# Two attention and dense layers on one core: a third query buffer, averages computed in pairs, and low parts moved to VectorE

## The chip, the core and the metric

The kernel runs on one core of a Trainium2 chip. The metric is the device time of one execution in microseconds; the figure for a version is the median of its runs. A core has a matrix engine, TensorE (PE, with its weight loads listed as PEld), and three engines for elementwise work, VectorE (DVE), ScalarE (ACT) and GpSimd (POOL). SyncE (SP) issues the DMA transfers between the memory off the core (HBM) and the core's own. Each engine takes its instructions in order and waits on semaphores for the others.

## What is computed

Two layers, each of two residual steps, on `x` of 2048 x 640 in fp32, with 32 heads of width 20 and a dense width of 1536:

```python
def _A_ref(x, wqkv, w_phi, wo):
    qkv = (x @ wqkv).reshape(B, S, 3, H, Dh) -> q, k, v per head
    pq = einsum("bhsd,hdf->bhsf", q, w_phi); pk likewise
    phi_q = concatenate([softmax(pq), softmax(-pq)], axis=-1)
    phi_k = concatenate([softmax(pk), softmax(-pk)], axis=-1)
    kv = einsum("bhsf,bhsd->bhfd", phi_k, v)
    z = sum of phi_k over s
    num = einsum("bhqf,bhfd->bhqd", phi_q, kv)
    den = einsum("bhqf,bhf->bhq", phi_q, z)[..., None] + 1e-6
    return (num / den) as rows @ wo

def _B_ref(x, w1, b1, w2):
    h = x @ w1 + b1
    return (h * tanh(softplus(h))) @ w2

x = x + _A_ref(_layernorm(x), ...)
x = x + _B_ref(_layernorm(x), ...)
(and the same two steps once more, with the same weights)
```

## The kernel before

**Numbers.** Each fp32 operand of a large matrix product is kept as a high part, its rounding to the matrix engine's format, and a low part, the rest (`operand - high`). A product is three matmuls: high by high, high by low weight, low by high weight. So every weight and every chunk of activations is split once: ScalarE copies the high part, another engine subtracts to get the low part. For weights that is `make_parts` (L152, subtraction at L155 on GpSimd), called by the generator `make_five` (L198), which gives out five row groups of weights one by one. For activations it is `Transposed.step` (copy and subtraction at L295 and L296 on VectorE), which gives two chunks of 128 columns at a time; `all()` does the steps that are left.

**Tiles and stages.** The rows go in 8 blocks (`NB`) of 2 tiles of 128 rows (`BT`). A layer has three stages.

1. `attend_first` (about 20 to 262 us in layer 1, 712 to 943 in layer 2). For each tile of rows it makes queries, keys and values. `queries` and `keys` project (L354), and `features` turns the result into the features: ScalarE copies it out of PSUM into a buffer `e`, VectorE finds a maximum and a minimum per head (L384), one subtraction is done on GpSimd for queries (L385) and on VectorE for keys, then come the exponential on ScalarE, the sum and its reciprocal on VectorE (L393, L394) and the scaling on GpSimd (L395). A query's features are transposed by VectorE (L439) and stored in HBM, `e_d`, by four DMAs on SP (L443). A key's features are multiplied with the values on PE and summed in one PSUM tile over all keys (L430).
   These generators are advanced a step at a time (`pending`, `advance`), so that the steps of several tiles interleave.
   The buffer `e` of a query comes from `query_tile`: two tiles, used in turn, in the place of weights that are not needed yet. The buffer of a key is one of the five `big` tiles (`big_tile`).
   Before the last block's fourth projection, `load(0)` starts the reading of block 0's query features into two `big` tiles (L548) and a smaller one.
2. `attend_second` (262 to 368 us, and 943 to 1051). `finish_kv` makes the summed products ready. For each tile, `average` multiplies the query features with them (L589, 44 matmuls, into a two-bank PSUM tile of `mm_tile`, of which there are two), and VectorE divides: sums to `den` (L598), their reciprocals (L599), the product (L602). The averaged rows of a block are turned by ten PE transposes (L290, within `Transposed.step`) and multiplied with `wo`: `Rows(b, t).half(c, ps)` is one half of the columns of one tile (15 matmuls, L354), after which VectorE adds the residual (L619) and takes statistics. PE and SP follow here the order in which the code is written (`manual_schedule`). The PSUM tiles of one bank come from `one_tile`, a ring of four.
3. `dense` (368 to 712 us, and 1051 to 1398). A step is a block and a pair of hidden chunks (six pairs a block): `hidden` (L697, 60 matmuls into a `one` tile) and `mish`, which is spread over ScalarE (L710, L714, L715, L722), VectorE (L712, L713, L717 to L721) and GpSimd (L723); some steps later `contract` (L739) multiplies its result with W2. In the first six steps the last five row groups of W2 are split, one a step (`last_w2`, L776). The normalized rows of the next block are read turned from HBM (`load_turned`) and split (`nxt.all()`) in the last step of a block.

**Order.** Outside stage 2 a scheduler with a model of time sets the order within each engine, bounded by the dependences, by the rings of buffers and by `issue_after`, which puts an instruction behind a named one. ScalarE's instructions that go through `act(...)` keep the order in which they are written.

Of the kernel before, what the change touches and what calls it, by code (L numbers as in the profile page):

```python
# [8 lines left out]
F32 = mybir.dt.float32  # L9
# [39 lines left out]
def kernel(  # L49
# [22 lines left out]
    def mm_tile():  # L72
        return psum.tile([P, 2, 512], F32, tag="mm", name="mm", bufs=2)
# [75 lines left out]
            c0 = c1  # L149
        return raw  # L150

    def make_parts(w, raw, ordered=False):  # L152
        for st, cs in raw:
            (act if ordered else nc.scalar.activation)(w[0][:, cs], st, AF.Copy)
            nc.gpsimd.tensor_tensor(w[1][:, cs], st, w[0][:, cs].bitcast(F32), op=ALU.subtract)  # L155

    def five_spares(j):

# [5 lines left out]
    def r2_wide(j, dtype=F32R):  # L164
        return wts.tile([P, 2, D], dtype, tag=f"r2{j}", name=f"r2{j}")
# [29 lines left out]
            nc.sync.dma_start(wp_d[1, s, k], kv_ws[k][s][:, :FW].bitcast(F32))  # L195
            nc.sync.dma_start(wp_d[0, s, k], q_ws[k][s][:, :FW].bitcast(F32))

    def make_five(j, rows):  # L198

        spares = five_spares(j)  # L200
        raws = [fetch_rows(rows(k), [spares[k]()]) for k in range(3)]
        yield
        for k in range(5):
            w = r2_pair(j + k)
            make_parts(w, raws[k])
            if k in (0, 1):
                raws.append(fetch_rows(rows(3 + k), [spares[3 + k]()]))
            yield w
# [156 lines left out]
        return g % 4, 2 * DH * (3 * (g // 4) + j)  # L365

    def query_tile(i):
        return r2_wide(10 + i % 2, F32).rearrange("p s d -> p (s d)")

    def features(ps, e, pool_sub):  # L370

# [197 lines left out]
    def attend_second(x_src, x_dst, acc, fetches, makes, fetch_next, begin_next):  # L569
        kva, o_ws, loaded, rest = acc  # L570
        rows = {}
        div = [None]

        def tail():

            with tc.issue_after(div[0]):
                next(rest, None)

        def average(b, t):

            phs = loaded[b]
            po = mm_tile()
            for g in range(G):
                n = 120 if g < 10 else 80
                w = GW if g < 10 else 42
                c, j = divmod(g, 8)
                for q in range(2):
                    s0 = t * P + 64 * q
                    nc.tensor.matmul(  # L589
                        po[64 * q:64 * q + 64, c, GW * j:GW * j + w], phs[g][:n, s0:s0 + 64],  # L590
                        kvb[:n, g, :w], start=True, stop=True)
            o = row_tile()
            den = work.tile([P, H], F32, tag="r", name="den", bufs=2)
            pv = [po[:, c, :(DH + 1) * n].rearrange("p (h d) -> p h d", d=DH + 1)
                  for c, n in ((0, 24), (1, 8))]
            hh = (slice(0, 24), slice(24, H))
            for c in range(2):
                nc.vector.tensor_scalar_add(den[:, hh[c]], pv[c][:, :, DH], DEN_EPS)  # L598
            nc.vector.reciprocal(den, den)  # L599
            for c in range(2):  # L600
                n = hh[c].stop - hh[c].start
                ins = nc.vector.tensor_tensor(o.rearrange("p (h d) -> p h d", d=DH)[:, hh[c]], pv[c][:, :, :DH],  # L602
                                        den[:, hh[c]].unsqueeze(2).to_broadcast([P, n, DH]), op=ALU.mult)
                div[0] = ins.ins
            rows.setdefault(b, []).append(o)
            if t == BT - 1:
                del loaded[b]

        class Rows:


            def __init__(self, b, t):
                self.t, self.xt, self.ps = t, xs[b], None
                self.bn = work.tile([P, 2, 6], F32, tag="bn", name="bn", bufs=2)

            def half(self, c, ps):
                project_half(ps, cur, self.t, o_ws, 0, c)
                part = self.xt[:, self.t, c * HC:(c + 1) * HC]
                nc.vector.tensor_tensor(part, ps[:, :HC], part, op=ALU.add)  # L619
                nc.vector.bn_stats(self.bn[:, c], part)  # L620

            def mean(self):
                mv = work.tile([P, 2], F32, tag="mv", name="mv", bufs=3)
                nc.vector.bn_aggr(mv, self.bn)
                return mv

        with tc.manual_schedule(engines={mybir.EngineType.PE, mybir.EngineType.SP}):
            kv = finish_kv(kva)
            next(rest)
            next(kv)  # L630
            loaded[1] = load(1)
            xs = {0: fetch(x_src, 0)}
            fetches[0]()
            next(rest)
            next(kv)
            next(rest)
            average(0, 0)
            average(0, 1)
            loaded[2] = load(2)
            average(1, 0)  # L640
            cur = Transposed(rows.pop(0)).all()
            average(1, 1)
            loaded[3] = load(3)
            for b in range(NB):
                if b == NB - 1:
                    ahead.all()
                elif b:
                    average(b + 1, 0)
                r0, r1 = Rows(b, 0), Rows(b, 1)
                r0.half(0, one_tile())  # L650
                if 0 < b < NB - 1:
                    average(b + 1, 1)
                tail()
                if b + 1 < NB:
                    xs[b + 1] = fetch(x_src, b + 1)
                if 0 < b and b + 3 < NB:
                    loaded[b + 3] = load(b + 3)
                if b == NB - 3:
                    fetch_next()
                r0.half(1, one_tile())  # L660
                mv0 = r0.mean()
                if b == NB - 2:
                    ahead = begin_next()
                py = mm_tile()
                r1.half(0, py[:, 0])
                if b + 1 < NB:
                    nxt = Transposed(rows.pop(b + 1)).all()
                r1.half(1, py[:, 1])
                norm_scale(b, [mv0, r1.mean()])
                xt = xs.pop(b)  # L670
                nc.sync.dma_start(row_block(x_dst, b), xt)
                makes[b]()
                if b + 1 < NB:
                    fetches[b + 1]()
                tail()
                if b < NB - 1:
                    cur = nxt
            for _ in rest:
                pass
        return ahead  # L680


    def dense(x_src, x_dst, w1s, w2s, first, last):
# [89 lines left out]
                ahead[t] = row_tile()  # L773
                nc.sync.dma_start(ahead[t], row_block(x_src, b)[:, t, :])

        last_w2 = make_five(KD, lambda k: w2[(7 + k) * P:(8 + k) * P, :])  # L776
        n_pr = KF // 2
        steps = [(b, pr) for b in range(NB) for pr in range(n_pr)]
        acts = {}
# [1 line left out]
        for i in range(len(steps) + SKEW):  # L781
            if i < len(steps):
# [5 lines left out]
                if pr == 3 and (b + 1 < NB or not last):  # L788
                    nxt = load_turned(n1_d[b + 1] if b + 1 < NB else n2_d[0], (v_tile, v_tile, row_tile))
                acts[i] = hidden(b, pr)  # L790
                if pr == 1 and b + 1 < NB:
                    with tc.issue_after(exps[0]):
                        normalize(b + 1, ahead, ahead)
                    spill_turned(ahead, n1_d[b + 1])
# [103 lines left out]
```

## Time and profile before

| | us |
|---|---|
| runs | 1399.83, 1400.14, 1402.13 |
| median | 1400.14 |
| the profiled execution | 1399.85 |
| its span | 1397.9 |
| its mean granted TensorE clock | 0.994 |

Busy time in the stages of the profiled execution, in us:

| stage | length | PE | DVE | ACT | POOL |
|---|---|---|---|---|---|
| layer 1, first phase (20 to 262) | 242 | 238.07 | 202.03 | 104.37 | 106.49 |
| second phase (262 to 368) | 106 | 105.09 | 79.67 | 27.98 | 40.08 |
| dense (368 to 712) | 344 | 342.32 | 274.60 | 171.87 | 90.49 |
| layer 2, first phase (712 to 943) | 231 | 220.08 | 201.10 | 89.95 | 103.36 |
| second phase (943 to 1051) | 108 | 107.33 | 79.79 | 28.46 | 40.79 |
| dense (1051 to 1398) | 347 | 340.73 | 243.23 | 156.69 | 75.49 |

The ends of the stages are read from where their first matmuls begin and are rounded. Times in rows of the profile are microseconds from the start of the span. A timeline row has the start, the duration, the engine, the line of the kernel, the operation, the tile written and the tiles read with their shapes, and how many instructions the row stands for; what is in brackets at its end is the idle time of the engine before it and what it waited for. A row of the waits has the engine, the tile and the line that waited, what it waited for, the total, the count and the longest. A row of the windows has busy time and count of each engine. A row of the groups has the busy time of all its instructions and the mean of one in ns.

### The profile page before, as it was taken

Reading aid. Unit: us, or ns where it says so; the run is one execution under the profiler, and the core shown is the slowest. Engines: PE = TensorE matmul, PEld = TensorE weight load, DVE = VectorE, ACT = ScalarE, POOL = GpSimd, SP = SyncE. Lnnn points to the kernel's source line nnn. Section 1 sums busy time; section 2 is a strip of 40 time slices with the busy share of each in tenths; the row PEclk is TensorE's granted clock in tenths of the full one; section 3 lists DMA queues with packets and bytes.
Section 4 is the critical chain, followed back from the end, with each engine's and each line's share of the span. In section 5 each row is a group of like instructions: output and inputs, shape, how many; then the busy total and the mean of one; then the engine's idle time right before and its main releaser. Section 6 shows DMA issues by size and latency. Waiting matters only on the chain. (4 is left out here: it accounts for less than half of the span.)

```text
span 1397.9 us, 30903 instructions
## 1 busy us (share of the span) xinstructions
PE 1364.9 (98%) x12866; PEld 1345.4 (96%) x12866; DVE 1089.6 (78%) x1814; ACT 587.7 (42%) x1035; POOL 460.1 (33%) x344
## 2 busy tenths in 40 slices
PE   7999999999999999999999999999999999999998
PEld 7989999999999999999999999989999999999998
DVE  5798877886688887788769899988667766777775
ACT  4444434222445454545443343432134544444443
POOL 1443543353442222222234544453344211211112
PEclk9999999999999999999999999999999999999999
DMA  8532434788624432344472433458965212333200
GB/s 312 156 60 63 88 51 93 201 242 290 207 62 95 114 96 65 73 107 104 137 229 56 91 67 58 67 118 268 279 236 177 74 26 71 95 95 95 68 28 20
DMA packets 350277, 169.03 MB, mean 121 GB/s; under 512 B 287097, under 2 KB 323689, under 8 KB 350137
## 3 DMA queue, kind: packets, MB, share of 16 engines
q1 hardware_dynamic: 350137, 167.06, 44.4%
q8 instruction: 101, 1.65, 0.5%
q14 instruction: 39, 0.32, 0.1%
HBM read 104.43 MB, written 62.59 MB: 119 GB/s over the span
## 5 line engine op out<-in xcount | busy, mean ns | idle before, releaser
L739 PE MATMUL mm<-r2h,ol 128*128 128x320 f32 x1280 | 305.4, 309 | 1.4 <-ACT ol L722 0.9
L723 POOL TENSOR_TENSOR ol<-big,ol 128x512 fp32r<-128x512 f32 (+1 forms) x98 | 130.6, 1333 | 458.1 <-ACT ol L722 393.0
L697 PE MATMUL one<-xtl,r1h 128*128 128x256 f32 x960 | 268.6, 280 | 2.0 <-DVE xtl L296 2.0
L697 PE MATMUL one<-xth,r1l 128*128 128x256 f32 x960 | 268.0, 279 | 0.0
L697 PE MATMUL one<-xth,r1h 128*128 128x256 f32 x960 | 266.5, 279 | 0.0
L739 PEld LDWEIGHTS mm<-r2h,ol 128*128 128x128 f32 x1280 | 219.1, 188 | 2.8 <-POOL ol L723 1.5
L739 PE MATMUL mm<-r2l,ol 128*128 128x320 f32 x640 | 197.3, 309 | 0.0
L354 PE MATMUL mm<-r1h,xth 128*128 128x304 f32 (+1 forms) x600 | 186.7, 311 | 6.8 <-ACT r L122 6.8
L354 PE MATMUL mm<-r1h,xtl 128*128 128x304 f32 (+1 forms) x600 | 185.4, 309 | 2.3 <-DVE xtl L296 2.2
L354 PE MATMUL mm<-r1l,xth 128*128 128x304 f32 (+1 forms) x600 | 185.5, 309 | 0.0
L697 PEld LDWEIGHTS one<-xtl,r1h 128*128 128x128 f32 x960 | 180.4, 188 | 2.7 <-DVE xtl L296 2.5
L697 PEld LDWEIGHTS one<-xth,r1l 128*128 128x128 f32 x960 | 180.4, 188 | 0.0
L697 PEld LDWEIGHTS one<-xth,r1h 128*128 128x128 f32 x960 | 179.9, 188 | 0.0
L712 DVE TENSOR_SCALAR big<-big 128x512 f32<-128x512 f32 (+1 forms) x98 | 56.6, 578 | 112.9 <-ACT big L710 112.9
L354 PE MATMUL mm<-r2h,xth 128*128 128x304 f32 (+1 forms) x460 | 142.6, 310 | 0.0
L354 PE MATMUL mm<-r2h,xtl 128*128 128x304 f32 (+1 forms) x460 | 140.4, 305 | 0.0
L354 PE MATMUL mm<-r2l,xth 128*128 128x304 f32 (+1 forms) x460 | 140.2, 305 | 0.0
L395 POOL TENSOR_TENSOR r<-r,r 128x1280 f32<-128x1280 f32 x32 | 77.5, 2423 | 149.0 <-DVE r L394 126.7
L354 PEld LDWEIGHTS mm<-r1h,xth 128*128 128x128 f32 x600 | 114.0, 190 | 8.1 <-ACT r L122 7.3
L710 ACT ACTIVATE big<-one,b1s 128x256 f32<-128x256 f32 x192 | 80.6, 468 | 96.2 <-PE one L697 95.6
L714 ACT ACTIVATE big<-big,two 128x512 f32<-128x512 f32 (+1 forms) x98 | 70.1, 715 | 119.2 <-DVE big L713 116.7
L739 PEld LDWEIGHTS mm<-r2l,ol 128*128 128x128 f32 x640 | 120.2, 188 | 0.0
(130 smaller groups left out, 3031.6 us busy)
## 6 DMA issues: line engine op xcount, KB each, us to landing
e_d<-r SPq DMA_DIRECT2D x128, 160.0 KB, 4.0
big<-e_d SPq DMA_DIRECT2D x32, 640.0 KB, 7.3
x_d<-xt SPq DMA_DIRECT2D x23, 640.0 KB, 4.0
xt<-x_d SPq DMA_DIRECT2D x22, 640.0 KB, 4.9
n_d<-xn SPq DMA_DIRECT2D x176, 80.0 KB, 2.4
xt<-in_x SPq DMA_DIRECT2D x16, 640.0 KB, 5.1
xn<-x_d SPq DMA_DIRECT2D x28, 320.0 KB, 4.2
v<-n_d SPq DMA_DIRECT2D x30, 256.0 KB, 3.2
```

What stands on the lines that cost most here:

```text
L354: nc.tensor.matmul(ps[:, :w], a[:, sl], r, start=(k == 0 and n == 0), stop=(k == KD - 1 and n == 2))
L395: nc.gpsimd.tensor_tensor(eg, eg, r.unsqueeze(2).to_broadcast([P, 2 * H, DH]), op=ALU.mult)
L697: nc.tensor.matmul(ph[:, j, :], l, r, start=(n == 0), stop=(n == 3 * KD - 1))
L710: exps[0] = nc.scalar.activation(part(ta, 0)[:, j - js.start], ph[:, j, :], AF.Exp, bias=b1s[:, 2 * pr + j:2 * pr + j + 1]).ins
L712: nc.vector.tensor_scalar_min(e, e, E_CAP)
L714: nc.scalar.activation(r, n, AF.Ln, bias=two)
L723: nc.gpsimd.tensor_tensor(al[:, js], n, ah[:, js].bitcast(F32), op=ALU.subtract)
L739: nc.tensor.matmul(pys[t][:, c, :HC], l[:, j, sl], r, start=(f == 0 and n == 0), stop=(f == KF - 1 and n == 2))
```

## The change

It has four parts.

1. `query_tile`: queries go round three buffers in place of two. The third is a `big` tile (query tiles 2, 5, 8, 11 and 14); the other two are the same as before.
2. `attend_second`: in the loop, the averages of both tiles of block b + 1 are computed one behind the other, ahead of the first half of block b; before, the second tile's stood between the first and the second half of `r0`. The two halves of `r1` take two `one` tiles; before, they took the two banks of an `mm` tile.
3. `make_parts` and `make_five` get an argument that names the engine of the low parts; `last_w2` has them made on VectorE, all others stay on GpSimd.
4. `dense`: in block 0, the first step of `nxt` (the split of block 1's first two chunks) is written at the fifth pair; before, it was done with the others at the sixth.

```diff
-    def make_parts(w, raw, ordered=False):
+    def make_parts(w, raw, ordered=False, low=nc.gpsimd):
         for st, cs in raw:
             (act if ordered else nc.scalar.activation)(w[0][:, cs], st, AF.Copy)
-            nc.gpsimd.tensor_tensor(w[1][:, cs], st, w[0][:, cs].bitcast(F32), op=ALU.subtract)
+            low.tensor_tensor(w[1][:, cs], st, w[0][:, cs].bitcast(F32), op=ALU.subtract)
...
-    def make_five(j, rows):
+    def make_five(j, rows, low=nc.gpsimd):
...
             w = r2_pair(j + k)
-            make_parts(w, raws[k])
+            make_parts(w, raws[k], low=low)
...
     def query_tile(i):
-        return r2_wide(10 + i % 2, F32).rearrange("p s d -> p (s d)")
+        return big_tile() if i % 3 == 2 else r2_wide(10 + i % 3, F32).rearrange("p s d -> p (s d)")
...
                 elif b:
                     average(b + 1, 0)
+                    average(b + 1, 1)
                 r0, r1 = Rows(b, 0), Rows(b, 1)
                 r0.half(0, one_tile())
-                if 0 < b < NB - 1:
-                    average(b + 1, 1)
                 tail()
...
                 mv0 = r0.mean()
                 if b == NB - 2:
                     ahead = begin_next()
-                py = mm_tile()
-                r1.half(0, py[:, 0])
+                r1.half(0, one_tile())
                 if b + 1 < NB:
                     nxt = Transposed(rows.pop(b + 1)).all()
-                r1.half(1, py[:, 1])
+                r1.half(1, one_tile())
...
-        last_w2 = make_five(KD, lambda k: w2[(7 + k) * P:(8 + k) * P, :])
+        last_w2 = make_five(KD, lambda k: w2[(7 + k) * P:(8 + k) * P, :], nc.vector)
...
                 acts[i] = hidden(b, pr)
+                if b == 0 and pr == n_pr - 2:
+                    with tc.issue_after(exps[0]):
+                        nxt.step()
                 if pr == 1 and b + 1 < NB:
```

## The prediction

> **What bounds the kernel now.** I read the page's first lines, then the waits of TensorE (PE) sorted by total, then busy time in windows of 20 us around each of those waits, then the chain of waits inside one block of the second phase. The page first:
>
> ```profile
> span 1397.9 us, 30903 instructions
> PE 1364.9 (98%) x12866; PEld 1345.4 (96%) x12866; DVE 1089.6 (78%) x1814; ACT 587.7 (42%) x1035; POOL 460.1 (33%) x344
> ```
>
> PE is busy for 98% of the span. So a gain has two sources: a stop of PE that goes away, or PE work that becomes cheaper. Idle time on the other engines counts only where it ends in such a stop. The waits of PE (engine, tile, line, releaser: us in total, times, longest) that stand near code of the change:
>
> ```profile
> PE mm L354 <- ACT r L122: 6.8, 2, 3.8
> PE one L430 <- POOL big L395: 3.9, 2, 3.2
> PE mm L354 <- DVE xtl L296: 2.2, 2, 1.8
> PE one L697 <- DVE xtl L296: 2.0, 2, 1.0
> ```
>
> That is 14.9 us. The windows say what else such a stop costs (columns: window, its length, busy us and instructions of PE, PEld, DVE, ACT, POOL, granted clock, DMA share, GB/s):
>
> ```profile
> 80.00:100.00 20.00, 16.97 (x222) 15.80 (x221) 19.92 (x25) 5.08 (x9) 10.93 (x8) 0.91 0.36 58
> 740.00:760.00 20.00, 19.59 (x254) 19.09 (x253) 20.00 (x22) 7.83 (x13) 11.42 (x6) 1.00 0.08 21
> 760.00:780.00 20.00, 16.23 (x222) 15.73 (x221) 15.83 (x17) 5.12 (x10) 9.02 (x5) 0.91 0.55 103
> 860.00:880.00 20.00, 20.00 (x249) 19.63 (x248) 19.32 (x21) 9.17 (x15) 6.59 (x4) 0.92 0.24 44
> 940.00:960.00 20.00, 18.48 (x373) 17.85 (x374) 14.02 (x36) 3.52 (x7) 3.54 (x3) 0.91 0.93 289
> 400.00:420.00 20.00, 18.76 (x141) 18.14 (x140) 15.38 (x22) 9.08 (x17) 6.16 (x5) 1.00 0.00 1
> 1080.00:1100.00 20.00, 18.71 (x137) 17.88 (x136) 14.87 (x20) 9.19 (x19) 8.22 (x6) 1.00 0.00 1
> ```
>
> The granted clock falls to 0.91 or 0.92 in or after the windows with the four longest stops and is 1.00 in the windows with the 1.0 us stops. A clock of 0.91 over 20 us is (1 - 0.91) x 20 = 1.8 us of PE lost besides the stop, 0.92 is 1.6. So a long stop costs its length and some 1.7 more. The reader should also see DVE busy for 20.00 and 19.92 us in two windows: ahead of those stops VectorE itself has no room.
>
> **Averages together (parts of the second phase).** The chain of waits inside one block there (start, duration, engine, tile, line, matmuls):
>
> ```profile
> 946.70 2.72 PE mm L589 x88
> ...
> 953.97 4.60 PE one L354 x30
> ...
> 961.86 2.20 PE mm L354 x15
> 964.06 1.41 PE mm L589 x44
> 965.47 2.40 PE one L354 x15
> 967.88 1.41 PE mm L589 x44
> 969.29 2.40 PE one L354 x15
> 971.68 2.20 PE mm L354 x15
> 973.89 1.09 PE one L290 x10
> ```
>
> A block is PE from end to end: 2.20 + 1.41 + 2.40 + 1.41 + 2.40 + 2.20 + 1.09 = 13.11 us. An average that stands alone is 1.41 and each projection half behind one is 2.40, while a half behind another is 2.20. Two averages in a row are 2.72 (the x88 row), two halves in a row 4.60 (the x30 row). The change makes it 2.20 + 2.72 + 4.60 + 2.20 + 1.09 = 12.81, so 0.30 less. Six blocks of a layer have averages in the loop, so 12 x 0.30 = 3.6 us, all on the path. Bounds: 0 if the switch between the two matmul shapes costs as much when it is done once, and 12 x 0.40 = 4.8 if each of the two places is worth the full difference of 2.40 to 2.20.
>
> The same part takes r1's two halves from the `one` ring, 7 tiles a block in place of 5, over 4 buffers. The second half then needs the tile that r1's first half used three allocations earlier, and waits for VectorE's add of that half (L619). VectorE's rows there:
>
> ```profile
> 305.04 0.49 DVE L619 TENSOR_TENSOR xt<-mm,xt 128x320 f32<-128x320 f32 x1 [0.94 <-PE mm L354]
> ...
> 310.43 0.89 DVE L602 TENSOR_TENSOR xn<-mm,den 128x480 f32<-128x480 f32 x2
> ```
>
> The add waits for PE, starts at once and takes 0.49; what hides it is the ten transposes between the halves, 1.09 us. I price this at nothing, with 0.6 us to spare (1.09 - 0.49). If that cover goes, everything behind the second half on PE (the next block's averages) waits too; that is the third rival.
>
> **Low parts on VectorE and the early split (start of the dense phase).** Rows of the first blocks of layer 1 against a later one:
>
> ```profile
> 400.38 1.94 DVE L713 SCALAR_TENSOR_TENSOR big<-big 128x512 f32<-128x512 f32 x1
> 408.65 1.80 POOL L155 TENSOR_TENSOR r2l<-xn,r2h 128x640 fp32r<-128x640 f32 x1 [0.63 <-POOL ol L723]
> 408.95 2.05 DVE L296 TENSOR_TENSOR xtl<-v,xth 128x512 fp32r<-128x512 f32 x1
> 417.12 0.69 DVE L713 SCALAR_TENSOR_TENSOR big<-big 128x512 f32<-128x512 f32 x1
> ```
> ```profile
> L134 DVE TENSOR_TENSOR r1l<-xn,r1h 128x640 fp32r<-128x640 f32 x4 | 3.3, 817 | 0.0
> ```
>
> A subtraction L155 on GpSimd is 1.80 us, and VectorE instructions that run beside one stretch: L713 takes 1.94 in place of 0.69, L296 2.05. L296 is the split of block 1's first chunks, and PE's hidden matmuls wait 1.0 us for it in each layer (the L697 row of waits). Moved to VectorE the subtraction is 0.82 by the row of L134, five a layer, 4.1 us; VectorE is busy 15.38 of 20 us in that window, so 4.6 are free. And the first split comes one step earlier. So the stop should go, and smaller delays of the activations with it. PE lacks 20 - 18.76 = 1.24 us in the one window and 20 - 18.71 = 1.29 in the other. I take 2.5 us for both layers, that is all of it, since both causes are taken away. Bounds: 0, if the activations' own chain sets the stop, and on the losing side 5 x 0.2 us, when each subtraction of 0.82 falls between two steps of one activation and its cover is short by a quarter, so +1.
>
> **The third query buffer (first phase).** Queries took two buffers in turn; a buffer is free when the transposed features are stored to HBM. ScalarE's copy out of PSUM waits for that store, and PE for ScalarE. The rows at the stops and those ahead of two others:
>
> ```profile
> 91.16 1.47 DVE L384 TENSOR_REDUCE m<-r 128x32 f32<-128x640 f32 x2
> 93.42 1.26 PE L430 MATMUL one<-big,v 128*21 128x40 f32 x56
> 93.69 1.27 POOL L385 TENSOR_TENSOR r<-r,m 128x640 f32<-128x640 f32 x1
> ...
> 770.00 0.68 ACT L122 ACTIVATE r<-mm 128x608 f32<-128x608 f32 x1 [8.91 <-DMA e_d<-r]
> 770.86 1.55 DVE L384 TENSOR_REDUCE m<-r 128x32 f32<-128x640 f32 x2 [1.88 <-ACT r L122]
> ...
> 831.22 1.54 DVE L384 TENSOR_REDUCE m<-r 128x32 f32<-128x640 f32 x2 [2.33 <-ACT r L122]
> ...
> 916.89 1.54 DVE L384 TENSOR_REDUCE m<-r 128x32 f32<-128x640 f32 x2 [2.16 <-ACT r L122]
> ...
> 941.08 2.26 PE L430 MATMUL one<-big,v 128*21 128x40 f32 x128 [3.18 <-POOL big L395]
> ```
>
> With a buffer to spare the copy no longer waits for the store. What is late next is VectorE and GpSimd, which make the features of queries and keys alike. Place by place:
> - Layer 1, at 87 to 90 us (3.03 of the 6.8 us): VectorE is busy 19.92 of 20 there. In the changed order query 3's reductions (1.47 us) and its GpSimd subtraction (1.27) stand ahead of the sum of key tile 2, which PE needs for L430. PE would reach that matmul some 3 us earlier than at 93.42 and find its operand 1.5 us later than before. The stop moves more than it goes: I take 0.5, bounds 4.8 (3.03 and the dip of 1.8) and -2 (a stop that is longer by 1.5, rounded up).
> - Layer 2, at 767 (3.8 us): VectorE is full up to 760 and idles 1.88 just ahead of 770.86. That much can be won; I take 2.0, bounds 5.6 (3.8 and 1.8) and 0.
> - Layer 2, at 856 to 858 (1.8 us, xtl of L296): VectorE idled 2.33 us at 831 for the copy and had not made it up by 858. Without that idle time the split is 2.33 earlier and the stop of 1.8 is gone, with the dip of 1.6 in the window from 860: 3.4, bounds 3.4 and 0.
> - Layer 2, at 938 (3.18 us, key features): VectorE idled 2.16 at 917. I take 2.0, bounds 5.0 (with its dip of 1.8) and 0.
>
> The Trainium skill, "TensorE: Matmul & The Clock Gate", section on the HAM clock gate, has the clock halved only after an idle window of about 3.4 us. By that rule the 1.8 us stop at 858 would have no dip, and the gain there would be 1.8 in place of 3.4; the row of 860 to 880 shows 0.92 all the same, and I go by the row.
>
> **What the borrowed buffer delays.** Query tiles 2, 5, 8, 11 and 14 now take one of the five `big` tiles, which keys and the loads of features for the second phase use as well. So the ring turns faster, and the two loads for block 1 (L548) get their tiles later; the first, on SP, now stands behind the last stores of a query and waits for the matmul of the last key tile. Before:
>
> ```profile
> 261.02 0.38 SPq L548 DMA_DIRECT2D big<-e_d  x1
> ...
> 267.36 0.80 PE L589 MATMUL mm<-kvb,big 120*64 120x63 f32 x20 [0.43 <-PE mm L589]
> ```
> ```profile
> big<-e_d SPq DMA_DIRECT2D x32, 640.0 KB, 7.3
> ```
>
> Only the second half was issued at 261.02 and landed 7.3 us later, at 268.3, just in time. Now both halves start then, with 640 KB more in flight; at the 289 GB/s of the window 940 to 960 that is 2.2 us. PE reaches the first average of block 1 at 267.36, so it waits 0 to 3 us. I take a loss of 1.0, bounds 0 and 8 (a stop of about 2.2 and a dip of 1.8 in each layer). In layer 2 the average of block 1 has more room and I add nothing.
>
> **The sum.** 3.6 + 2.5 + 0.5 + 2.0 + 3.4 + 2.0 - 1.0 = 13.0 us off the profiled execution, which took 1399.85 (span 1397.9 and 1.95 around it): 1386.9. The median of the three runs is 1400.14, so 0.3 above; my forecast for the median is 1387.0.
>
> **The rivals.**
> - *The wait only changes its name.* VectorE bounds the first phase (20.00 and 19.92 busy), so that the third buffer lets ScalarE run ahead and PE stops as long for key features and splits. For it: the two windows. Against: VectorE's idle times of 1.88, 2.33 and 2.16, all for the copy. Then 3.6 + 2.5 - 1.0 = 5.1 remain: 1395.
> - *All stops vanish.* The four stops with their dips are 3.0 + 1.8, 3.8 + 1.8, 1.8 + 1.6 and 3.2 + 1.8 = 18.8; with 3.6 and 2.5 that is 24.9: 1375. Against: the full window up to 760, and GpSimd's place in the order of layer 1.
> - *Slower: r1's second half waits for its tile.* If VectorE's add of the first half stands behind both averages' divisions (two tiles by 0.89 and their smaller steps, some 3 us), the half stops for 3 + 0.49 - 1.09 = 2.4 us in each of 12 blocks, 29 us, and the time is 1416. It decides from 1.1 us a block (13 / 12). Against: the divisions can start as the averages end, and 4.60 + 2.20 us of halves come before that add.
> - *It doesn't do what it says:* the copies already had other reasons to wait. The releaser in the rows, the store of `e_d`, speaks against it; its time is that of the first rival.
>
> **How the numbers follow.** The forecast has 0.56, with a range of its own of 1382 to 1391; the wait that changes its name 0.22; all stops vanish 0.13; slower 0.09. A change under 0.2% (2.8 us) can't be told from none. The forecast and the third case are faster by more, and 0.15 of the first rival's 0.22; the rest of it, 0.07, is the same. So faster 0.84, same 0.07, slower 0.09. The range runs from 1378, half way into the case without stops, to 1397, past the first rival; it leaves out some 0.15.
>
> **What would show it.** In the profile after: averages as rows of x88 and halves as x45 in a block of 12.8 us; no wait of ScalarE for `e_d` at the four places; at 90 us a PE stop of some 3 us at L430 in place of L354; no wait of L697 for xtl at 410 and 1092, L713 near 0.7 at 400; windows after 860 at clock 1.00; a short wait for `big<-e_d` at 267. The forecast is wrong if PE's waits in the first phase keep their total, if L354 waits for L619 in the second phase, or if the averages' rows grow with their number.

## The result, and the profile after

| | before | after |
|---|---|---|
| median of the runs, us | 1399.99 (4 runs, 1398.67 to 1402.13) | 1382.85 (4 runs, 1381.50 to 1384.39) |
| span of the profiled execution, us | 1397.9 | 1380.6 |

The ratio is 0.9876, with a 95% interval of 0.9859 to 0.9894. That is 17.1 us less, where 13 were forecast; the time lies inside the range of 1378 to 1397. From here on, lines of the kernel after are two lower than before from the loop of `attend_second` on (L697 is L695, L713 is L711).

The page after, and the waits of TensorE (PE) near the changed code:

```profile
span 1380.6 us, 30853 instructions
PE 1356.1 (98%) x12866; PEld 1341.1 (97%) x12866; DVE 1082.9 (78%) x1824; ACT 586.5 (42%) x1035; POOL 442.0 (32%) x334
```
```profile
PE mm L354 <- DVE xtl L296: 3.6, 5, 1.4
PE mm L354 <- ACT xth L122: 2.6, 1, 2.6
PE one L430 <- POOL big L395: 1.6, 2, 0.9
PE mm L589 <- DMA big<-e_d: 0.8, 1, 0.8
```

The wait for ScalarE's copies of queries (6.8 us before) is gone, and so is that of the hidden matmuls for xtl, the low part of a chunk of activations (2.0). ScalarE's own 16 waits for the stores to `e_d` (74.9 us before) are gone too. The wait for a key's features is 1.6 in place of 3.9. New are 2.6 us for xth, the high part of a chunk; the projections' wait for xtl grew from 2.2 to 3.6 us, and that for a load from 0.2 to 0.8. So PE's stops of the first phases (for query copies, key features, xtl and xth) fell from 12.9 to 7.8 us and did not go. To find where the 17 us come from, take three matmuls that stand at the same place of both programs: the last product of keys and values of layer 1, the first projection of layer 2, and the last product of layer 2. First before, then after (timeline of PE; the row for 941.08 of before is in the prediction):

```profile
260.12 1.48 PE L430 MATMUL one<-big,v 128*21 128x40 f32 x128 [0.68 <-POOL big L395]
713.69 0.71 PE L354 MATMUL one<-r1h,xth 128*128 128x320 f32 x3 [1.50 <-ACT r1h L133]
```
```profile
262.08 1.48 PE L430 MATMUL one<-big,v 128*21 128x40 f32 x128 [0.68 <-POOL big L395]
711.36 0.71 PE L354 MATMUL one<-r1h,xth 128*128 128x320 f32 x3 [1.51 <-ACT r1h L133]
929.85 1.48 PE L430 MATMUL one<-big,v 128*21 128x40 f32 x128 [0.94 <-POOL big L395]
```

| stretch | before | after | difference |
|---|---|---|---|
| start to the last product of layer 1 | 260.12 | 262.08 | +1.96 |
| to the first projection of layer 2 (second phase and dense) | 453.57 | 449.28 | -4.29 |
| to the last product of layer 2 (first phase) | 227.39 | 218.49 | -8.90 |
| to the end of the span (second phase and dense) | 456.82 | 450.75 | -6.07 |

The four sum to -17.3, the difference of the spans. Layer 1's first phase became longer; all else became shorter. (Of the 1.96 us, 0.40 were there by the 300th projection matmul, at 77.42 and 77.82 us. That start varies from 75.90 to 77.82 us over all profiles here, so 1.6 us are left for the change.) The windows that stood in the prediction, after the change (columns as there):

```profile
80.00:100.00 20.00, 16.54 (x211) 15.18 (x210) 18.02 (x24) 4.37 (x9) 11.96 (x8) 0.83 0.30 48
760.00:780.00 20.00, 18.07 (x243) 17.33 (x242) 18.83 (x21) 5.99 (x11) 9.09 (x5) 1.00 0.55 104
860.00:880.00 20.00, 20.00 (x143) 20.00 (x142) 18.88 (x20) 8.35 (x16) 11.71 (x6) 1.00 0.49 86
380.00:400.00 20.00, 20.00 (x160) 20.00 (x159) 19.09 (x31) 12.65 (x24) 4.96 (x4) 1.00 0.53 135
400.00:420.00 20.00, 20.00 (x151) 20.00 (x150) 16.20 (x25) 9.82 (x19) 4.64 (x4) 1.00 0.01 2
```

At 80 to 100 us the granted clock is 0.83 where it was 0.91; in layer 2 it is 1.00 where it was 0.91 and 0.92. At the start of the dense phase PE has no idle time left. In layer 1 PE's idle time from 80 to 100 us is 3.46 us where it was 3.03; what it loses more there is mainly clock, 3.4 us in place of 1.8 ((1 - 0.83) x 20 and (1 - 0.91) x 20). One block of the second phase, in the chain of waits after:

```profile
962.25 2.20 PE one L354 x15
964.45 2.70 PE mm L589 x88
967.15 6.80 PE one L354 x45
973.95 1.09 PE one L290 x10
```

That is 12.79 us, where it was 13.11 and 12.81 were forecast. And the place that got worse, 87 to 92 us in layer 1, from the timeline after:

```profile
87.64 1.53 DVE L384 TENSOR_REDUCE m<-r 128x32 f32<-128x640 f32 x2
...
89.55 0.92 DVE L387 TENSOR_TENSOR big<-m,big 128x640 f32<-128x640 f32 x1
89.75 2.94 POOL L395 TENSOR_TENSOR big<-big,r 128x1280 f32<-128x1280 f32 x1
90.40 2.38 DVE L272 SCALAR_TENSOR_TENSOR stats<-mv,stats 128x1 f32<-128x1 f32 x2
90.57 1.27 ACT L122 ACTIVATE big<-big 128x1280 f32<-128x1280 f32 x1 [7.44 <-DVE big L387]
91.74 0.37 ACT L122 ACTIVATE xth<-one 128x256 fp32r<-128x256 f32 x1
...
92.16 0.41 PE L354 MATMUL mm<-r1h,xth 128*128 128x304 f32 x1 [2.64 <-ACT xth L122]
```

Read from the bottom: PE waits for xth; ScalarE, which keeps its written order, makes xth behind the exponential of key 3; that exponential waits for VectorE's L387; and ahead of L387 stand 1.53 us of reductions for query 3, whose copy the third buffer let through early. Two tiny instructions L272 then take 2.38 us on VectorE; that is looked at below.

### The profile page after: what moved, and what is told of

Its sections match the earlier page's. It is cut to its first block, busy times and chain, and to the rows that moved or that the text cites. A ratio compares the mean times of both kernels' runs of the same rounds, so it can differ in the third digit from the quotient of the medians.

```text
span 1380.6 us, 30853 instructions
## 1 busy us (share of the span) xinstructions
PE 1356.1 (98%) x12866; PEld 1341.1 (97%) x12866; DVE 1082.9 (78%) x1824; ACT 586.5 (42%) x1035; POOL 442.0 (32%) x334
## 4 chain that ended last, share of the span: by engine, by line
PE 83%; DVE 6%; DMA 2%; POOL 1%; issue 1%; ACT 1%; SPq 0%; DVEq 0%; POOLq 0%; ACTq 0%
PE one L695 24%; PE mm L737 24%; PE mm L354 18%; PE one L354 11%; PE mm L589 3%; PE one L290 2%; PE one L430 1%; DVE r L393 1%; DVE m L384 1%; DMA big<-e_d 1%; DVE xtl L296 1%; DVE r L439 1%; DVE big L387 1%; DVE big L385 1%; POOL big L395 1%
## 5 line engine op out<-in xcount | busy, mean ns | idle before, releaser
L695 PE MATMUL one<-xtl,r1h 128*128 128x256 f32 x960 | 268.2, 279 | 0.0
L695 PE MATMUL one<-xth,r1l 128*128 128x256 f32 x960 | 268.0, 279 | 0.0
L695 PE MATMUL one<-xth,r1h 128*128 128x256 f32 x960 | 265.9, 279 | 0.0
L695 PEld LDWEIGHTS one<-xtl,r1h 128*128 128x128 f32 x960 | 180.4, 188 | 0.0
L695 PEld LDWEIGHTS one<-xth,r1l 128*128 128x128 f32 x960 | 180.4, 188 | 0.0
L695 PEld LDWEIGHTS one<-xth,r1h 128*128 128x128 f32 x960 | 179.6, 188 | 0.0
L395 POOL TENSOR_TENSOR big<-big,r 128x1280 f32<-128x1280 f32 x42 | 102.7, 2445 | 82.9 <-DVE r L394 58.4
L354 PEld LDWEIGHTS mm<-r1h,xtl 128*128 128x128 f32 x600 | 113.6, 189 | 4.8 <-DVE xtl L296 4.7
L720 ACT ACTIVATE ol<-big 128x512 fp32r<-128x512 f32 (+1 forms) x98 | 60.9, 621 | 134.4 <-DVE big L719 134.3
L354 PEld LDWEIGHTS mm<-r1l,xth 128*128 128x128 f32 x600 | 113.5, 189 | 0.2
```

What stands on the lines that cost most here:

```text
L354: nc.tensor.matmul(ps[:, :w], a[:, sl], r, start=(k == 0 and n == 0), stop=(k == KD - 1 and n == 2))
L395: nc.gpsimd.tensor_tensor(eg, eg, r.unsqueeze(2).to_broadcast([P, 2 * H, DH]), op=ALU.mult)
L695: nc.tensor.matmul(ph[:, j, :], l, r, start=(n == 0), stop=(n == 3 * KD - 1))
L720: nc.scalar.activation(ah[:, js], n, AF.Copy)
```

## The experiments

**The four parts, each alone on the kernel before.** Their edits are the four parts of the diff above.

`q3_alone` is part 1 (`query_tile` alone):

> Before with part 1 alone (third query buffer). Theory, from the two profiles: layer 1's first phase becomes 2.6 us longer (the stop at 87 to 92 us stays and moves from the copy that waits for e_d to the copy of block 2's last chunk, which stands on ScalarE behind a key's exponential), layer 2's first phase 10.4 us shorter, and the first averages of each layer wait some 0.5 us for their load; in sum -7.3, about 1392.7. Rival: the gain of layer 2's first phase needs the other parts too (another order, earlier loads); then this kernel gains less than 4 us.

`avg_alone` is part 2 (the averages and the tiles of `r1`):

> Before with part 2 alone (averages of two tiles together, r1 in single-bank tiles). Theory: 0.30 us less in each of 12 blocks, x88 rows of 2.70 and x45 rows of 6.80, no wait of L354 for the add L619: -3.6, about 1396.4. Rival: r1's second half waits for its tile, the loop is 1 us or more longer per block and the time is not below before.

`low_alone` is part 3 (`make_parts`, `make_five`, `last_w2`):

> Before with part 3 alone (low parts of W2's last rows on VectorE). Theory: a VectorE instruction with two operands in SBUF stands still while GpSimd runs an elementwise one; without GpSimd's five subtractions L713 is 0.7 and L296 0.7 us, so the split of block 1's first chunks comes 1.4 us sooner and the stop of 1.0 us at L697 goes without the early split: -2.9 in each layer, about 1394.2. Rival: the stop needs the early split; then this part gives -1.7 a layer (about 1396.6) and L697 still waits for xtl.

`split_alone` is part 4 (the three lines in `dense`):

> Before with part 4 alone (first split of block 1 a step sooner). Theory: the stop of 1.0 us at L697 goes in both layers, L713 stays at 1.9 us where GpSimd subtracts, and 1.2 us a layer are gained: about 1397.7. Rival: the early split itself stands beside a GpSimd subtraction and delays the activation's instructions on VectorE, so that no more than 0.5 us in all is gained.

| part alone | median, us | against before (1399.83) | ratio, 95% interval |
|---|---|---|---|
| q3_alone | 1393.52 | -6.3 | 0.9946 to 0.9975 |
| avg_alone | 1396.33 | -3.5 | 0.9964 to 0.9985 |
| low_alone | 1394.42 | -5.4 | 0.9951 to 0.9977 |
| split_alone | 1398.58 | -1.3 | 0.9986 to 1.0005 |

The differences of the medians sum to 16.5 of the 17.1 us, the ratios to 14.7 us; with some 2 us of uncertainty in each part, that agrees with parts that hardly depend on one another, but doesn't show it. The traces show it better, by the time between the same two matmuls of two programs. From the first average in the second phase's loop to the last ten transposes (six blocks) PE takes 78.63 us in each layer before, and 76.71 (76.70 in layer 2) after; `avg_alone` has 76.71 in both layers, the other three parts 78.62 or 78.63. From those ten transposes to block 1's first hidden matmul:

| | before | after | low_alone | split_alone |
|---|---|---|---|---|
| layer 1 | 360.62 to 452.00: 91.38 | 361.21 to 449.66: 88.45 | 359.93 to 448.47: 88.55 | 358.55 to 449.54: 91.00 |
| layer 2 | 1042.62 to 1134.05: 91.43 | 1028.30 to 1116.43: 88.13 | 1040.40 to 1128.61: 88.21 | 1041.04 to 1131.78: 90.74 |

The third buffer does by itself what it does in the whole change; its windows show both sides, the loss in layer 1 and the clock of 1.00 from 860 on:

```profile
80.00:100.00 20.00, 16.77 (x213) 15.42 (x212) 18.02 (x24) 4.92 (x9) 11.40 (x8) 0.83 0.32 52
860.00:880.00 20.00, 20.00 (x166) 19.94 (x153) 19.06 (x22) 8.95 (x15) 7.77 (x4) 1.00 0.37 64
```

In `low_alone` the stop at L697 is gone without the early split. Its timeline where block 1 is split:

```profile
402.75 0.69 DVE L713 SCALAR_TENSOR_TENSOR big<-big 128x512 f32<-128x512 f32 x1
403.35 0.69 DVE L296 TENSOR_TENSOR xtl<-v,xth 128x512 fp32r<-128x512 f32 x1
```

With GpSimd's subtraction away, L713 and L296 take 0.69. In `split_alone`, where it is still on GpSimd, the first chunks are split early, and the stop only moves to the last chunk, which now stands beside the subtraction:

```profile
406.82 2.08 POOL L155 TENSOR_TENSOR r2l<-xn,r2h 128x640 fp32r<-128x640 f32 x1 [0.94 <-POOL ol L723]
...
407.40 1.77 DVE L296 TENSOR_TENSOR xtl<-xn,xth 128x256 fp32r<-128x256 f32 x1
...
409.23 0.39 PE L697 MATMUL one<-xtl,r1h 128*128 128x256 f32 x1 [0.73 <-DVE xtl L296]
```

So part 4 alone gives 0.4 and 0.7 us by the table of the two stretches (the interval of its time includes no change), where its theory had 1.2 in each layer and the stop gone. Where part 3 is in, the same table leaves 0.1 us a layer for it (88.55 to 88.45 and 88.21 to 88.13).

**Layer 1 without the third buffer.**

```diff
-    def query_tile(i):
+    def query_tile(i, layer):
+        if layer == 0:
+            return r2_wide(10 + i % 2, F32).rearrange("p s d -> p (s d)")
```

> After, but the third query buffer in layer 2 alone; layer 1 goes round two as before. Theory: in layer 1 the third buffer only lets query 3's reductions stand ahead of key 3's features on VectorE, so without it the first phase of layer 1 is 2 to 2.6 us shorter and the wait of the first average for big<-e_d is gone in layer 1; layer 2 keeps its gain: 1382.85 - 2.5, about 1380.3. Rival: the 2.6 us were a difference between two executions; then the time stays at 1382.9 within 0.8.

The median was 1380.43 (ratio to before 0.9847 to 0.9877), 2.4 us under the kernel after, as the theory said; none of its four runs is as long as any of the kernel after. In its profile the last product of layer 1 is back near its place of before (259.10). In this order of work, the third buffer costs in layer 1 and wins in layer 2.

**Layer 1 with it, in another order on VectorE.** `last_sub[0]` is the last subtraction of the last key whose features were written; `behind` holds for query 3 of layer 1 alone.

```diff
         for s, op in ((0, ALU.max), (1, ALU.min)):
-            nc.vector.tensor_reduce(m[:, s], eh[:, 1], axis=AX.X, op=op)
+            with tc.issue_after(last_sub[0]) if behind else nullcontext():
+                nc.vector.tensor_reduce(m[:, s], eh[:, 1], axis=AX.X, op=op)
```

> After, with the two reductions of query 3 in layer 1 held behind key 3's last subtraction on VectorE. Theory: the stop at 89 to 92 us comes from these 1.5 us of VectorE work standing ahead of the key's features, behind whose exponential ScalarE's copy xth stands; the stop shrinks from 2.8 to 1.3 us and with it the window's loss of clock (0.83): 2 to 4 us off, 1379 to 1381. Rival: VectorE is full there and the same work only comes later: the stop turns up at the next matmul that needs a split or a key, and less than 1 us is gained.

1379.00 us (0.9832 to 0.9865), 3.9 us under the kernel after: the theory's upper end. The matmul that waits, and the window:

```profile
90.22 0.40 PE L354 MATMUL mm<-r1h,xth 128*128 128x304 f32 x1 [1.02 <-ACT xth L122]
```
```profile
80.00:100.00 20.00, 18.86 (x298) 17.55 (x300) 20.00 (x26) 6.42 (x12) 10.97 (x8) 1.00 0.33 54
```

The stop is 1.0 us in place of 2.6, and the clock of the window 1.00 in place of 0.83. From the 300th projection matmul to the last product, layer 1's first phase takes 179.5 us, against 184.3 in the kernel after and 182.7 before. So the same work costs less when it comes later, although VectorE is full there, and with this order the third buffer wins in layer 1 too. It is the order of two pieces of VectorE work, and not its total, that made layer 1 longer.

**Why a 128x1 instruction takes 2.3 us.** L272 of the kernel before stands at 88.39 as well. What these long instructions share is seen at another one, the split that PE waited for at 858 in the kernel before:

```profile
855.69 2.36 POOL L395 TENSOR_TENSOR big<-big,r 128x1280 f32<-128x1280 f32 x1 [1.42 <-DVE r L394]
856.85 1.49 DVE L296 TENSOR_TENSOR xtl<-xn,xth 128x256 fp32r<-128x256 f32 x1
```

GpSimd's instruction ends at 855.69 + 2.36 = 858.05 and VectorE's at 856.85 + 1.49 = 858.34. The same split of 128x256 takes some 0.35 to 0.41 us elsewhere. So it looks as if it began only when GpSimd had ended. In the rows above for the kernel after, L395 ends at 89.75 + 2.94 = 92.69 and the pair of L272 at 92.78. If so, it should matter how many of VectorE's operands are tensors in SBUF, where all on-core tiles of this kernel lie but PE's results, which go to PSUM. The new form of L272 has one, and takes the other column as a scalar for each row:

```diff
-            nc.vector.scalar_tensor_tensor(stats[:, b, 1, t:t + 1], mvs[t][:, 0:1], -1.0,
-                                           stats[:, b, 0, t:t + 1], op0=ALU.mult, op1=ALU.mult)
+            nc.vector.tensor_scalar(stats[:, b, 1, t:t + 1], mvs[t][:, 0:1], -1.0, stats[:, b, 0, t:t + 1],
+                                    op0=ALU.mult, op1=ALU.mult)
```

> After, with L272 (128x1) written as tensor_scalar with a per-partition scalar in place of scalar_tensor_tensor. Theory: a VectorE instruction with two tensor operands in SBUF cannot begin before GpSimd's running elementwise instruction ends, which is why L272 takes 2.31 us at 90.4 in layer 1 and ends with GpSimd's L395; with one tensor operand it takes 0.15, VectorE is 2.1 us earlier there and the second stop of that place (1.1 us) goes: 1 to 2.5 us off, about 1381. Rival: the small instruction waits for GpSimd in either form (2.3 us), and nothing changes.

1379.55 us (0.9842 to 0.9872), 3.3 us under the kernel after, more than the 1 to 2.5 that were expected. The timeline:

```profile
87.83 5.85 POOL L395 TENSOR_TENSOR big<-big,r 128x1280 f32<-128x1280 f32 x2
88.47 0.32 DVE L272 TENSOR_SCALAR stats<-mv,stats 128x1 f32<-128x1 f32 x2
...
89.18 2.27 DVE L387 TENSOR_TENSOR r<-m,r 128x640 f32<-128x640 f32 x1
```

The two L272 take 0.32 us together beside the same GpSimd instruction. The next one with two operands, L387, now takes 2.27 (it took 0.75 in the kernel after) and ends at 91.45. GpSimd's first L395 there ends at 90.77, and 0.68 us later L387 is done. So the form of the instruction decides, and the wait passed to the next one of that form. What that is worth in time is not shown: PE's stop for xth stays 2.6 us, the second one behind it shrinks from 0.8 to 0.5, where the theory had it go. By the 300th projection matmul and the last product, layer 1's first phase takes 183.0 us against 184.3, and the clock alone accounts for that: the window from 80 to 100 us lost two portions of 1.7 us in the kernel after (0.83) and one here (0.91).

The Trainium skill, "SBUF — State Buffer", section "Who interferes with whom", says that a VectorE instruction with two SBUF inputs and a GpSimd one that reads SBUF hold a shared port in turn, each for its whole length. The sums of starts and durations above agree: 858.05 against 858.34, and the 0.29 us between them are a little less than the split's own time.

**Both edits, and shorter GpSimd instructions.** `behind_key_and_scalars` has the last two edits together:

> After, with both: query 3's reductions behind key 3's features, and L272 as tensor_scalar. Theory: with the first edit alone PE's stops at 89 to 92 us are 1.2 and 0.3 us at full clock and L272 stands 0.86 us; so the second can take no more than some 0.5 us on top: 1378.5, against 1379.0 with the first alone. Rival: the gains of 3.9 and 3.3 add up: 1375.7.

1376.95 us (0.9824 to 0.9850), between the theory's 1378.5 and the rival's 1375.7: 2 us less than the first edit alone, where at most 0.5 were expected. The runs of the two overlap (1375.95 to 1379.15 and 1377.50 to 1380.84). In the profiles PE's wait for xth is 1.0 us as with the first edit, and from the 300th projection matmul to the last product layer 1's first phase takes 179.4 us against 179.5. So the second edit adds nothing at the place where it should; the gains of 3.9 and 3.3 don't add up.

`scaling_in_halves` is that kernel with the scaling in two:

```diff
-        nc.gpsimd.tensor_tensor(eg, eg, r.unsqueeze(2).to_broadcast([P, 2 * H, DH]), op=ALU.mult)
+        for g in (slice(0, H), slice(H, 2 * H)):
+            nc.gpsimd.tensor_tensor(eg[:, g], eg[:, g], r[:, g].unsqueeze(2).to_broadcast([P, H, DH]), op=ALU.mult)
```

> The kernel before this one (query 3 behind key 3, L272 as tensor_scalar), with GpSimd's scaling of the features (L395, 128x1280) as two instructions of 128x640. Theory: VectorE's instructions with two tensor operands in SBUF stand until the GpSimd instruction that runs has ended, so their longest durations shrink with it: the key subtraction L387 from 2.75 us at most to 2.0 or less, its mean of 0.8 to 1.1 by some 0.2; PE's stops of 1 to 1.6 us in the first phases shrink by some 1 us in all, about 1377.5. Rival: the two engines share a bandwidth; then the same instructions are slowed by the same amount in sum and the durations stay, and GpSimd's second instruction costs 0.1 us each, so the time stays or rises by up to 1 us.

1374.86 us (0.9810 to 0.9837), the lowest median of all kernels here, 8 us under the kernel after and 2.1 under its own base; the interval overlaps with that of the base. Layer 1's first phase takes 177.1 us by the same two matmuls, in place of 179.4. The groups of L296 by shape (busy, mean ns), first with the scaling in one piece, then in halves:

```profile
L296 DVE TENSOR_TENSOR xtl<-one,xth 128x512 fp32r<-128x512 f32 x52 | 34.0, 679 | 3.5 <-ACT xth L122 3.2
L296 DVE TENSOR_TENSOR xtl<-xn,xth 128x512 fp32r<-128x512 f32 x14 | 17.2, 1227 | 0.0
```
```profile
L296 DVE TENSOR_TENSOR xtl<-one,xth 128x512 fp32r<-128x512 f32 x52 | 33.9, 678 | 3.7 <-ACT xth L122 3.3
L296 DVE TENSOR_TENSOR xtl<-xn,xth 128x512 fp32r<-128x512 f32 x14 | 10.6, 760 | 0.0
```

`one` is a PSUM tile, `xn` one of SBUF. The split with one operand from PSUM takes 679 and 678 ns; with both in SBUF the same shape took 1227, and 760 once GpSimd's instructions were half as long. The rival, a shared bandwidth, would have left the durations. The key subtraction, for which the expectation was made, shrank less: its mean from 1007 to 898 ns (0.2 us were expected), its longest from 2.98 to 1.90 us (2.0 or less was expected). PE's waits in the projections for xtl and xth are no longer in the list.

**How long r1's second half can wait.** Part 2 was priced on the claim that the half waits for VectorE's add of the first one, under a cover of 0.6 us. `longer_adds` puts more work ahead of that add (statistics whose results nobody uses; `more` is a count for the block, 1, 2, 4, 6 and 8 in layer 1):

```diff
-            def half(self, c, ps):
+            def half(self, c, ps, extra=0):
...
+                for _ in range(extra):
+                    ins = nc.vector.bn_stats(junk, ps[:, :HC])
+                with tc.issue_after(ins.ins) if extra else nullcontext():
...
-                r1.half(0, one_tile())
+                r1.half(0, one_tile(), more.get(b, 0))
```

> After, with 1, 2, 4, 6, 8 (layer 1, blocks 1 to 5) and 3, 5, 7, 0, 10 (layer 2, blocks 1 to 5) extra statistics instructions on VectorE, some 0.43 us each, whose results nobody uses, ahead of the add of r1's first half. Theory: the ten transposes cover 1.09 - 0.49 = 0.6 us, so one extra instruction costs nothing, and n of them stop PE for 0.43 n + 0.49 - 1.09 us: 0.3, 1.1, 2.0, 2.8 and 0.7, 1.6, 2.4, 0, 3.7; stops from some 1.8 us on are followed by 1.7 us lost in the clock: in sum 14.6 and 4 to 5 times 1.7, about 1404. Rival 1: with no cover at all every instruction costs 0.43 us (20 us without the clock). Rival 2: the clock only falls after stops of 3.4 us, which is the last one alone: 1399.

One execution took 1394.81 us, and not 1404: the expectation was wrong. The block with four extra instructions:

```profile
322.04 0.69 DVE L296 TENSOR_TENSOR xtl<-one,xth 128x512 fp32r<-128x512 f32 x1
...
322.79 0.41 PE L354 MATMUL one<-r2h,xth 128*128 128x320 f32 x1 [0.76 <-DVE xtl L296]
...
324.38 0.47 DVE L626 TENSOR_TENSOR xt<-one,xt 128x320 f32<-128x320 f32 x1
```

PE starts r1's second half at 322.79, though the add of the first one (L626) runs only at 324.38. The half waited for L296 of the new block's first chunks: it got the tile of those transposes, not that of r1's first half. So in this block the four `one` tiles are not handed out in turn. Why is not shown; it may be that the build, which models the time of each engine, picks the tile that it expects to be free first. The waits of PE in the five blocks of layer 1:

```profile
PE one L354 <- DVE xtl L296: 2.3, 3, 0.8
PE one L354 <- DVE xt L626: 0.4, 1, 0.4
```

One extra instruction shows no wait, as the cover of 0.6 us has it (the block takes 12.95 us in place of 12.79); two cost 0.4 us of waiting for the add itself (0.3 was expected; the block takes 13.48); four, six and eight all cost 0.8, for the split (13.81). In layer 2 one wait was 2.6 us, where a query's transpose stood on VectorE between the splits. So the third rival's 2.4 us in each block is not borne out: where the add is late, the half takes another tile.

`pairs_in_mm_tile` takes the other sub-edit of part 2 back:

```diff
-                r1.half(0, one_tile())
+                py = mm_tile()
+                r1.half(0, py[:, 0])
...
-                r1.half(1, one_tile())
+                r1.half(1, py[:, 1])
```

> After, but r1's two halves share an mm tile as before, the averages staying together. Theory: the second average of the next block then waits for VectorE's add of r1's second half, which is done 0.55 us after the half ends, while the first average takes 1.36: no stop, x88 rows of 2.7 us, and the time stays at 1382.9 within 0.8, so the single-bank tiles are no part of the gain. Rival: the tile of r1 waits for a division of the averages that stands late on VectorE, a stop of 0.5 us or more in each of 12 blocks: 1389 or more.

1383.99 us (0.9875 to 0.9902 against before; the kernel after has 0.9859 to 0.9894). The intervals overlap. In the traces two blocks of each layer are longer, 13.32 and 13.14 us in layer 1, and the list has PE waiting for VectorE's add L619 (0.8 us in three waits); the other four take 12.79. The six blocks take 77.52 and 77.53 us, against 76.71 in the kernel after and 78.63 before. So the rival of 0.5 us in each block is out, and the theory that the single-bank tiles are no part of the gain is out as well: of 1.92 us a layer, 1.1 come from the averages' pairing and 0.8 from the tiles.

## Why the prediction was right, and where it was not

| term of the sum | forecast | measured |
|---|---|---|
| averages in pairs | -3.6 | -3.8 (2 x (76.71 - 78.63)) |
| low parts and early split | -2.5 | -6.2 (88.45 - 91.38 and 88.13 - 91.43) |
| queries, layer 1 | -0.5 | +1.6 (184.3 - 182.7) |
| queries, layer 2 | -7.4 | -10.4 (235.75 - 246.16) |
| later load | +1.0 | +0.9 |

The last column is the time between the same two matmuls in the profiles of before and after. For layer 2's queries these are the last hidden matmul of layer 1 (700.47 and 698.13) and the first average of layer 2 (946.63 and 933.88); for the load, the first average of a layer and the first one of the loop (17.82 to 18.37 and 17.36 to 17.72). With 0.4 us at the start and 0.3 in the last dense phase, which no term has, the column gives the 17.3 us of the spans. The sum of the forecast came near it partly by luck: it was 2.1 us too favourable for layer 1's queries, and 3.7 and 3.0 us too cautious for the dense phase and for layer 2's queries.

**Averages.** Right in size: 12.79 us a block against 12.81. The sum had all of it from the pairing; by `pairs_in_mm_tile` 0.8 of the 1.92 us a layer need the single-bank tiles. The mechanism of the cover was right in the kernel after (no wait for L619 in the list), but the reason given, a ring in which the half must have that one tile, was not, as `longer_adds` shows.

**Dense phase.** Right in mechanism; the term was mis-sized. It counted the idle time of PE in one window of each layer (1.24 and 1.29 us), and between the same two matmuls the stretch became 2.93 and 3.30 us shorter. A row of before shows what that leaves out:

```profile
380.00:400.00 20.00, 19.57 (x150) 19.17 (x149) 17.74 (x25) 11.49 (x21) 11.21 (x7) 1.00 0.59 149
```

PE lost time in the window ahead as well: busy 19.57 us with 150 matmuls, where the row of after has 20.00 with 160. The two windows hold partly different work, but 0.43 us of busy time stand against 10 matmuls of 0.125 us each (20 / 160); busy time alone hides part of the loss. The early split, to which the prediction gave a share, hardly mattered: `low_alone` has no stop at L697 and 2.83 and 3.22 us of the gain.

**Queries in layer 2.** At 856 to 858 the 3.4 us came as forecast: the stop is gone and the window from 860 has clock 1.00. At 767 and 938 the stops shrank about as forecast (3.8 to 1.9 in two pieces, 3.2 to 0.9), but the step that failed is that the dips of the clock, 1.7 us each, were kept there. In the profile after, both places have clock 1.00, and that is about the 3.0 us between 7.4 and 10.4. At 767 this is partly luck: eight profiles here have the same two stops (0.5 and 1.4 us) at that place, and in three of them (`q3_alone`, `q3_behind_key`, `stats_two_scalars`) a dip follows.

**Queries in layer 1.** Wrong in sign. That it lies inside the bounds (a loss of 2) is luck: they were made from a longer stop, and the loss is in the main a second portion of the clock's dip. The prediction saw query 3's reductions stand ahead of key work on VectorE and looked for the new stop at L430, behind key 2's sum. It came at the projection ahead of it (92.16), since ScalarE's xth is ordered behind key 3's exponential. `q3_behind_key` shows the cause: with that order alone turned, the stop is 1.0 us and the kernel 3.9 us faster.

**The load.** The first average of block 1 waits 0.8 us for `big<-e_d` in layer 1 (0.2 before); layer 2 has no such row, though the stretch there is 0.4 us longer. Together that is close to the 1.0 taken.

**The rivals.** "The wait only changes its name" is what happened at one of the four places, in layer 1, where VectorE was full. "All stops vanish" came true for one of the three others, that at 856. The slower case didn't come, and when `longer_adds` forced the late add, a block became 1.0 us longer at most, but for one.

## What to carry to other kernels

Where two elementwise engines work side by side, look first at instructions that are much longer than their equals and end with an instruction of the other engine. A shorter instruction there, a form with one tensor operand, or the move of the work to one engine can be worth more than its own duration; the move was worth 6 us here. An extra buffer moves work forward on in-order engines; look at what it then stands ahead of, on each of them. To say what an edit is worth, take the time between the same two instructions of both programs: here it repeats to within 0.1 us where medians differ by 2.

## What was not expected of the hardware

The clock's dips come in portions, and these lie on a grid. The trace's record of the granted clock, between 20 and 1365 us of the thirteen profiles, has two values alone, 1.0 and 0.5. Each stretch at 0.5 is 3.41 us long, or two of these in a row (6.83), which costs 1.7 or 3.4 us of PE. In the kernel before they start at 91.60, 770.85, 859.60 and 941.52 us: 199, 26 and 24 times 3.413 us apart. Windows cut on the grid show what lies ahead of a dip, for the kernel before, the kernel after and `q3_alone`:

```profile
856.19:859.60 3.41, 1.58 (x11) 1.33 (x10) 2.15 (x3) 0.33 (x1) 3.27 (x2) 1.00 0.85 146
859.60:863.01 3.41, 3.41 (x82) 3.11 (x84) 2.88 (x4) 1.33 (x4) 1.27 (x1) 0.50 0.23 79
```
```profile
764.94:768.35 3.41, 1.96 (x13) 1.46 (x11) 3.41 (x7) 0.57 (x1) 2.49 (x1) 1.00 0.94 145
768.35:771.76 3.41, 2.94 (x21) 2.94 (x22) 3.41 (x4) 0.65 (x3) 3.41 (x3) 1.00 0.88 144
```
```profile
770.47:773.88 3.41, 1.74 (x10) 1.49 (x11) 3.41 (x6) 0.83 (x2) 3.41 (x2) 1.00 0.90 136
773.88:777.29 3.41, 3.41 (x16) 3.41 (x15) 3.41 (x3) 0.10 (x1) 3.41 (x3) 0.50 0.80 150
```

PE idles 1.83, 1.45 and 1.67 us in the first row of each pair, and the clock falls in the first case and the third. The second and the third are the same two stops of 0.5 and 1.4 us, which the grid cuts differently. Over all such windows that themselves ran at full clock, half clock followed each of the 16 in which PE idled 2.1 us or more, 8 of the 16 with 1.47 to 2.01 us, and none with less. So the same stop may or may not have a dip, by where on the grid it falls. What decides between 1.47 and 2.01 us stays open.

The Trainium skill, "TensorE: Matmul & The Clock Gate", section on the HAM clock gate, has a window of about 3.4 us that runs freely, and a halved clock after an idle one. The grid of 3.41 us agrees with the first; with the second the traces don't, since windows with half their length idle were followed by dips too.
